# Two chunks of the first batch taking turns by groups of blocks, with sequence sums kept in DRAM between turns

## The chip, the cores and the metric

One core of a Trainium2 chip runs the whole kernel. The metric is the device time of an execution in microseconds (us); a median is over the runs named beside it.

Engines: PE multiplies matrices, PEld loads its weights, DVE is the vector engine, ACT the scalar engine, POOL is GpSimd, SP issues most transfers.

## The reference

A Fourier filter along the sequence, then a gated feed-forward block:

```python
X = np.fft.rfft(x, axis=1)                      # x: (8, 3008, 256) float32
y = np.fft.irfft(X * (filt_r + 1j * filt_i)[None], n=3008, axis=1).astype(np.float32)
h = y.reshape(8 * 3008, 256)
g = h @ w_gate                                  # (256, 1536), float64
silu = g * (1.0 / (1.0 + np.exp(-g)))
return (silu * (h @ w_val) @ w_out).astype(np.float32)
```

The weights arrive as 64-bit floats, 3 x 3.1 MB.

## The kernel before: the parts that matter

For each of 8 batches the kernel does the filter as matrix products (stage 1, stage 2, and stage 3, which writes y) and then the feed-forward block in 12 steps. A step is one chunk k (of 4, in sequence) with one group g (of 3) of the hidden units. In the schedule, tokens such as `Q0`, `A01`, `E23` are groups of products on weights or on sums of weights, and `t0.1` and the like are pieces of the filter for later chunks and the next batch, slipped in between. `t4` is what stage 3 of a chunk reads back from DRAM (tile `t`); `f`, `c` and `m` are copies that ACT makes of PE's results and that PE or DVE needs to go on. The products `A`, `B`, `E` multiply sums of sequence parts ("sequence sums", the tile `y_t`) with sums of weights, so each change of chunk needs new sums, and each change of group other weights.

The 64-bit weights are turned into float32 in 36 half-blocks, one per *round*. A round works on half-block i and finishes half-block i-1:

```python
def round_half(i):
    raw = raws[i]                                 # 128 x 2 x 128 pairs of 32-bit words
    pw = ...; w = ...                             # ring buffers
    DVE: w  = high word & 0xFFFFF                 # "the mask"
    DVE: pw = (high word >> 20) & 0x7FF
    ACT: w, pf, pf, pw                            # four operations, 0.42 to 0.51 us each
    load_weights(i + NRAW - 1)                    # issued by ACT
    yield
    DVE: pw = sign bits | pw;  w = low word * 2**-52 + w
    POOL: products w * pf into the weight tile, then sums of them    # KERNEL BEFORE

def round_next():
    first half of round i, then second half of round i-1
```

(This is shortened; names and order are the kernel's.) Before the steps begin, 17 rounds are done; steps 0, 1 and 2 of the first batch carry 6, 10 and 4 more. Each group of the finished weights is stored to DRAM (3.3 MB) so that later chunks and batches can load them again.

## Time and profile before

| | before |
|---|---|
| time, median of 3 runs | 3012.14 us (3010.92 to 3012.99) |
| PE busy | 97% |
| first feed-forward product (`wk`) starts at | 100.2 us |
| PE restarts after its last long gap at | 125.2 us |
| steps 0, 1, 2, 3, 4 of batch 0 | 53.9, 48.5, 38.8, 30.3, 30.3 us |
| end of step 4 | 302 us |

A step with PE at its limit takes 30.3 us; only the first 241 us have anything to give.

### The profile page before, as it was taken

The page shows a single profiled execution, that of the slowest core. Times are in us where ns is not written, and L with a number is a line of the kernel's source. Part 1 is how long each engine was busy: PE and PEld are TensorE (multiplying, and loading weights), DVE is VectorE, ACT ScalarE, POOL GpSimd, SP SyncE. Part 2 cuts the span into 40 slices and gives each one's busy share as a digit, 9 for nine tenths or more (in the row PEclk, how much of TensorE's full clock was granted, in tenths as well). Part 3 has the DMA queues.
Part 4 walks back from the last instruction along what each step waited for, and adds up shares of the span by engine and source line. Part 5 has one row for each costly group of instructions (what it writes and reads, how often), then busy time and mean ns, then how long its engine had stood idle before and what let it go on. Part 6 is the DMA issues. An engine that isn't in the chain of part 4 may idle for free.

```text
span 3008.6 us, 57532 instructions
## 1 busy us (share of the span) xinstructions
PE 2930.9 (97%) x20286; PEld 2836.1 (94%) x20286; DVE 1920.6 (64%) x4385; ACT 1627.2 (54%) x4206; POOL 1578.4 (52%) x1763
## 2 busy tenths in 40 slices
PE   7589999999999999999999999999999999999999
PEld 5479999999999999999999999999999999999999
DVE  5675676566765666557665576655676566766665
ACT  6565555555555555555555545555545555555554
POOL 3664645455645455546554556544655445654453
PEclk8789999999999999999999999999999999999999
DMA  8445665556655656456655575556664556544442
GB/s 218 138 169 184 214 199 165 185 186 194 212 165 179 207 188 213 150 186 207 198 174 184 173 227 184 182 171 194 197 215 156 188 186 202 193 161 145 139 135 90
DMA packets 203849, 545.53 MB, mean 181 GB/s; under 512 B 28992, under 2 KB 99760, under 8 KB 202704
## 3 DMA queue, kind: packets, MB, share of 16 engines
q1 hardware_dynamic: 153002, 466.50, 48.6%
q10 hardware_dynamic: 41632, 51.46, 5.2%
q0 software_dynamic: 8928, 23.89, 2.6%
q8 instruction: 163, 2.67, 0.4%
q14 instruction: 124, 1.02, 0.1%
HBM read 459.68 MB, written 82.05 MB: 180 GB/s over the span
## 4 chain that ended last, share of the span: by engine, by line
PE 92%; DVE 0%; ACT 0%; issue 0%; POOL 0%; ACTq 0%
PE wa L626 24%; PE wA L703 17%; PE wk L626 16%; PE we L626 12%; PE wG L703 8%; PE wF L703 4%; PE pd L548 3%; PE pa L465 3%; PE pb L505 2%; PE pc L532 2%; DVE o L219 0%; DVE pw L284 0%; DVE y L226 0%; DVE h L222 0%; DVE h L219 0%
## 5 line engine op out<-in xcount | busy, mean ns | idle before, releaser
L626 PE MATMUL wa<-y_t,wt_t 128*128 128x188 f32 x4560 | 900.1, 323 | 5.8 <-ACT m L661 2.7
L626 PEld LDWEIGHTS wa<-y_t,wt_t 128*128 128x128 f32 x4560 | 747.0, 190 | 31.2 <-issue 15.2
L626 PE MATMUL wk<-y,wt_t 128*128 128x188 f32 x3040 | 583.0, 325 | 34.2 <-ACT f L641 24.0
L219 POOL TENSOR_TENSOR h<-h 128x376 f32<-128x376 f32 x190 | 182.7, 984 | 815.9 <-DVE h L673 815.9
L703 PE MATMUL wA<-wo_t,h 128*128 128x128 f32 x4608 | 579.8, 276 | 3.7 <-DVE o L219 2.7
L703 PEld LDWEIGHTS wA<-wo_t,h 128*128 128x128 f32 x4608 | 565.1, 192 | 16.9 <-issue 12.0
L222 POOL TENSOR_TENSOR h<-h 128x376 f32<-128x376 f32 x570 | 553.0, 994 | 0.5
L626 PEld LDWEIGHTS wk<-y,wt_t 128*128 128x128 f32 x3040 | 491.9, 191 | 63.8 <-ACT f L641 25.4
L222 DVE TENSOR_TENSOR we<-we,m 128x376 f32<-128x376 f32 x576 | 319.0, 556 | 202.4 <-PE we L626 145.5
L626 PE MATMUL we<-y_t,wt_t 128*128 128x188 f32 x2280 | 440.5, 323 | 0.0
L626 PEld LDWEIGHTS we<-y_t,wt_t 128*128 128x128 f32 x2280 | 377.5, 190 | 0.1
L222 POOL TENSOR_TENSOR D<-f,f 128x376 f32<-128x376 f32 x288 | 280.2, 986 | 110.0 <-ACT f L641 109.3
L226 DVE SCALAR_TENSOR_TENSOR y<-wk,c 128x376 f32<-128x376 f32 x480 | 244.5, 543 | 141.0 <-ACT we L657 87.0
L661 ACT COPY m<-wa 128x376 f32<-128x376 f32 x576 | 272.2, 473 | 89.9 <-PE wa L626 88.8
L668 ACT ACTIVATE g<-wa 128x188 f32<-128x188 f32 x576 | 188.3, 327 | 196.1 <-PE wa L626 188.4
L703 PE MATMUL wG<-wo_t,h 128*128 128x128 f32 x2304 | 289.5, 276 | 0.6 <-DVE o L219 0.6
L703 PEld LDWEIGHTS wG<-wo_t,h 128*128 128x128 f32 x2304 | 282.7, 192 | 0.8 <-DVE o L219 0.8
L668 ACT ACTIVATE u<-we 128x188 f32<-128x188 f32 x576 | 189.3, 329 | 168.2 <-DVE we L222 149.2
L641 ACT ACTIVATE f<-wk 128x376 f32<-128x376 f32 x288 | 139.7, 485 | 242.2 <-PE wk L626 223.3
L645 ACT COPY c<-wk 128x376 f32<-128x376 f32 x288 | 136.1, 473 | 227.4 <-PE wk L626 227.2
L648 DVE SCALAR_TENSOR_TENSOR x<-wk,f 128x376 f32<-128x376 f32 x192 | 104.4, 544 | 236.8 <-PE wk L626 236.2
L657 ACT COPY we<-y 128x376 f32<-128x376 f32 x480 | 223.6, 487 | 31.3 <-DVE h L673 12.9
(128 smaller groups left out, 3856.3 us busy)
## 6 DMA issues: line engine op xcount, KB each, us to landing
wt_t<-w_all SPq DMA_DIRECT2D x186, 896.0 KB
wt_t<-w_all SPq DMA_DIRECT2D x186, 768.0 KB
t<-d SPq DMA_DIRECT2D x64, 384.0 KB
d<-t ACTq DMA_DIRECT2D x112, 192.0 KB
lent<-de_tbl SPq DMA_DIRECT2D x84, 256.0 KB
lent<-in_filt_r_dram SPq DMA_DIRECT2D x336, 64.0 KB
lent<-d SPq DMA_DIRECT2D x84, 256.0 KB
d<-lent ACTq DMA_DIRECT2D x84, 256.0 KB
```

The source lines that it names most:

```text
L219: return eng.tensor_tensor(out=dst, in0=a, in1=b, op=ALU.add)
L222: return eng.tensor_tensor(out=dst, in0=a, in1=b, op=ALU.subtract)
L226: return nc.vector.scalar_tensor_tensor(out=dst, in0=a, scalar=-1.0, in1=b, op0=ALU.mult, op1=ALU.subtract)
L465: pin(nc.tensor.matmul(out=ps[0:NK], lhsT=wf_t, rhs=self.x.pop(u), start=True, stop=True))
L626: pin(nc.tensor.matmul(out=ps[:, z], lhsT=self.wt[:, SLOT[p], z], rhs=rhs, start=start and z == 0, stop=True, skip_group_check=True))
L641: pin(act.mul(self.small(f"f{i}", f"f{i}", 1), t[f"k{i}"], -1.0))
L645: pin(act.copy(out=self.small(f"c{i}", f"c{i}", 1), in_=t[f"k{i}"]))
L648: pin(v.scalar_tensor_tensor(out=dst, in0=t[f"k{j}"], scalar=-1.0, in1=t[f"f{i}" if j == 3 else f"D{at}"], op0=ALU.mult, op1=ALU.add))
L657: pin(act.copy(out=self.bank(f"e{at}"), in_=t[f"y{at}"]))
L661: pin(act.copy(out=self.small(f"m{at}", "m", 4), in_=t[f"a{at}"]))
L668: pin(act.activation(out=self.small(op, "g", 3, 1)[:, 0], in_=ps[:, 1], func=AF.Silu))
L703: pin(nc.tensor.matmul(out=self.tiles[at][:, t, :], lhsT=self.hs[i][:, HID[p], t0:t0 + 128], rhs=wo_t[:, JB * q + i, WO[p], :], start=star ...
```

## The change

The intent: between two changes of weights there are now two steps instead of one, because chunks 0 and 1 use each group in turn. So group 1 is needed one step later and group 2 two steps later, fewer rounds have to be done before the first step (10 calls in place of 17), and the rest spread evenly (6, 6, 6, 6, 3). The price is that the sequence sums of the two chunks, which share one tile, are stored and loaded again at each turn.

```diff
-    xpool = pool("xp", 3)
+    xpool = pool("xp", 2)
-    NRAW = 3
-    N_EARLY = 16
+    NRAW = 2
+    N_EARLY = 15
-        pw = rpool.tile(..., tag="pw", bufs=2)
+        pw = rpool.tile(..., tag="pw", bufs=3)
-        pin(e.tensor_tensor(out=y, in0=w[:, 1], in1=pf[:, 1], op=ALU.mult))       # e is POOL
+        pin(v.tensor_tensor(out=y, in0=w[:, 1], in1=pf[:, 1], op=ALU.mult))       # v is DVE
  ... (the other two products likewise)
-            if u < N_TWO:                      # real filter part doubled by two ACT copies
+            if u < N_TWO and u % 3:            # four of twelve blocks: two half products on DVE
-        idle(tb0..., [bank("idle") for _ in range(4)], 512)
-        for _ in range(4):
+        for _ in range(2):
             round_next()
  ... (rounds inside the filter loop and behind it: 2 + 1 in place of 5;
       just before the first step 1 in place of 4)
+    yt_dram = [wdpool.tile([128, 3 * len(PAIRS), TQ], FP32, name=f"yt_{k}") for k in range(2)]
+    def keep_sums(k, d):
+        pin(nc.sync.dma_start(out=sums_of(yt_dram[k], d), in_=sums_of(y_t, d)))
+    def reload_sums(k, d):
+        pin(nc.sync.dma_start(out=sums_of(y_t, d), in_=sums_of(yt_dram[k], d)))
+    for d in (2, 1, 3):
+        keep_sums(0, d)                        # behind four weight stores, all on SP
+        if b == 0:
+            steps[:2 * NG] = [(k, g) for g in range(NG) for k in range(2)]
-                if step in (0, 2, 5):
+                chunk = ({0: 1, 2: 2, 5: 3} if b else {0: 1, 3: 2, 6: 3}).get(step)
  ... (t4 of that chunk is loaded at the start of the step)
```

Cut: the new tables of which round, weight sum and filter piece goes to which token, the output tile's second buffer, and the order in which half-blocks are taken.

More of the change, by code (lines that the diff above doesn't have):

```diff
@@ L191, in weights_of @@
     def weights_of(b, k, g):
-        return wt_1 if (b, k, g) == (0, 0, 1) else wt_t
+        return wt_1 if b == 0 and k < 2 and g == 1 else wt_t
     dram_tiles = [wdpool.tile([2 * NS, N2, C], FP32, name=f"d{1 + i % 2}_{i // 2}")
                   for i in range(4)]
+    yt_dram = [wdpool.tile([128, 3 * len(PAIRS), TQ], FP32, name=f"yt_{k}") for k in range(2)]
     w_dram = wdpool.tile([NG, 128, NPR, 2, 128], FP32, name="w_all")
@@ L250, in weight_halves @@
                 yield from hid(g, i)
-            for j in range(JB * (g - 1), JB * g) if g else ():
+            for j in range(JB * g, JB * g + JB):
                 yield from proj(j)
-        for j in range(JB * (NG - 1), NJ):
-            yield from proj(j)
     weights = list(weight_halves())
     raws = {}
-    NRAW = 3
-    N_EARLY = 16
+    NRAW = 2
+    N_EARLY = 15
     def load_weights(i):
@@ L275, in round_half @@
         low, high = raw[:, :, :, 0], raw[:, :, :, 1]
-        pw = rpool.tile([128, 2, 128], U32, name=f"pw_{i}", tag="pw", bufs=2)
+        pw = rpool.tile([128, 2, 128], U32, name=f"pw_{i}", tag="pw", bufs=3)
         w = rpool.tile([128, 2, 128], FP32, name=f"w_{i}", tag="w", bufs=2)
@@ L304, in round_half @@
             dst = wo_t[:, j]
-            pin(e.tensor_tensor(out=dst[:, ts(l, 2), :], in0=w, in1=pf, op=ALU.mult))
+            pin(v.tensor_tensor(out=dst[:, ts(l, 2), :], in0=w, in1=pf, op=ALU.mult))
             if l:
@@ L315, in round_half @@
         x, y, u = w[:, 0], wt[:, SLOT[f"Q{i}"], z], wt[:, SLOT[f"P{i}"], z]
-        pin(e.tensor_tensor(out=y, in0=w[:, 1], in1=pf[:, 1], op=ALU.mult))
-        pin(e.tensor_tensor(out=x if KS[i] else u, in0=x, in1=pf[:, 0], op=ALU.mult))
+        pin(v.tensor_tensor(out=y, in0=w[:, 1], in1=pf[:, 1], op=ALU.mult))
+        pin(v.tensor_tensor(out=x if KS[i] else u, in0=x, in1=pf[:, 0], op=ALU.mult))
         if KS[i] == -1:
@@ L356, in reload_weights @@
         tc.keep_in_program_order(nc.sync.dma_start(out=wt_t[:, a:b], in_=w_dram[g, :, a:b]))
-    PREPARE = {(0, "B03"): [("k", 1, p) for p in range(4)], (1, "B03"): [("k", 2, 0)],
-               (2, "A01"): [("k", 2, p) for p in (1, 2, 3)]}
-    for step, tokens in ((0, "Q0 P3 P0 Q2 A01 B01"), (1, "Q0 P3 P1 A13 P2 B13 Q3 A12 B02 B12"),
-                         (2, "A13 P2 B01 A02")):
+    PREPARE = {(2, "B03"): [("k", 1, p) for p in range(4)], (4, "B03"): [("k", 2, p) for p in range(4)]}
+    for step, tokens in ((0, "Q1 P1 A13 B13 A12 E13"), (1, "Q0 P1 A01 Q3 E12 A23"),
+                         (2, "Q0 P1 A01 Q3 E12 A23"), (3, "Q0 P1 A01 Q3 E12 A23"),
+                         (4, "Q2 B13 E12")):
         for token in tokens.split():
             PREPARE.setdefault((step, token), []).append("r")
-    for g, pairs in ((1, "0Q313 0A0201 0A1202 0B0212 0B1223 0A2303"),
-                     (2, "1A0213 1E1201 1E0202 2Q112 2P123 2Q203")):
+    for g, pairs in ((1, "1E2313 1B0301 2P302 2P012 2P223 2B0103"),
+                     (2, "3E2313 3B0301 4P302 4P012 4P223 4B0103")):
         for p in pairs.split():
@@ L466, in stage1 @@
                                          start=True, stop=True))
-            self.load_x(u + 3)
+            self.load_x(u + 2)
             yield
@@ L510, in stage2a @@
             v = nc.vector
-            fr, fi = (f[:, 0], f[hi, 1]) if self.b else (self.real.pop(u), f[hi])
-            pin(v.tensor_tensor(out=pt, in0=ps, in1=fr, op=ALU.mult))
+            fi = f[hi, 1] if self.b else f[hi]
+            if self.b or u in self.real:
+                fr = f[:, 0] if self.b else self.real.pop(u)
+                pin(v.tensor_tensor(out=pt, in0=ps, in1=fr, op=ALU.mult))
+            else:
+                for h in (lo, hi):
+                    pin(v.tensor_tensor(out=pt[h], in0=ps[h], in1=f[lo], op=ALU.mult))
             pin(v.scalar_tensor_tensor(out=qt[lo], in0=ps[hi], scalar=-1.0, in1=fi,
@@ L571, in stage3, with sums_of @@
                         out=v, in0=b, scalar=-float(k), in1=c, op0=ALU.mult, op1=ALU.add))
+    def sums_of(t, d):
+        a = SUM[f"A0{d}"]
+        return t.rearrange("p (e s) n -> p e (s n)", e=3)[:, :, a * TQ:(a + 4 - d) * TQ]
     def combine_sequence(y, d, v=nc.gpsimd):
@@ L679, in step @@
                 if self.following:
-                    combine_sequence(self.following(), i)
+                    self.following(i)
         def project(self, op, last=False):
@@ L709, in project @@
                 outs[b, k] = [opool.tile([128, len(TOK), C], FP32, name=f"o{i}_{b}_{k}",
-                                         tag=f"o{i}") for i in range(2)]
+                                         tag=f"o{i}", bufs=2) for i in range(2)]
             i, cb = {1: (0, 0), 2: (0, 0), 6: (0, 1), 3: (0, 1), 4: (1, 0), 7: (1, 1),
@@ L757, in early_raw @@
             t = wt_t[:, spare[i]:spare[i] + 2].rearrange("p s z f -> p (s z f)") if i < 8 else \
-                wo_f[:, ts(i - 8, 512)]
+                wo_f[:, JB * 7 * 128 + 512 * (i - 8):JB * 7 * 128 + 512 * (i - 7)]
             return t.bitcast(U32).rearrange("p (b f two) -> p b f two", b=2, two=2)
@@ L776 @@
                 round_next()
-        idle(tb0.rearrange("p s k c -> p (s k c)"), [bank("idle") for _ in range(4)], 512)
         for u in range(2):
@@ L791 @@
                 run(spec.stage2b(u - lag))
-            if 2 < u < 11:
+            if u in (2, 5):
+                round_next()
+            if 2 < u < 9:
                 load_weights(len(raws))
@@ L796 @@
     following = Spectral(1)
-    for u in range(3):
+    for u in range(2):
         following.load_x(u)
-    for _ in range(3):
-        round_next()
+    round_next()
     for i, j in PAIRS:
         combine_weights(0, i, j)
-    for _ in range(2):
-        round_next()
     warm()
@@ L811 @@
         keep_weights(0, piece)
-    for _ in range(4):
-        round_next()
+    round_next()
+    def keep_sums(k, d):
[4 more added lines that the diff above has]
+        keep_sums(0, d)
     hpool = pool("hp", 4)
@@ L822, with order_of, sequence_of, make @@
     pieces_before = []
+    def order_of(b):
+        steps = [divmod(step, NG) for step in range(NCHUNK * NG)]
+        if b == 0:
+            steps[:2 * NG] = [(k, g) for g in range(NG) for k in range(2)]
+        return steps
+    def sequence_of(cur, nxt, step):
+        steps = order_of(cur.b)
+        if step + 1 == len(steps):
+            return (lambda d: combine_sequence(nxt.y[0], d)) if nxt else None
+        k, after = steps[step][0], steps[step + 1][0]
+        if k == after:
+            return None
+        if cur.b == 0 and 0 < step < 2 * NG - 1:
+            return lambda d: reload_sums(after, d)
+        def make(d):
+            combine_sequence(cur.y[after], d)
+            if cur.b == 0 and step == 0:
+                keep_sums(after, d)
+        return make
     for b in range(B):
@@ L846 @@
             plan[10], plan[11] = two[21:24], three(nxt, 0)
+            if b == 0:
+                plan[0], plan[1] = d[0] + one[0:1], one[1:6]
+                plan[4] = [iter(()), iter(())] + two[0:3]
+                plan[5], plan[6] = d[1] + two[3:4], two[4:9]
+                plan[7] = two[9:10] + d[2]
+                plan[8], plan[9], plan[10] = two[10:15], two[15:20], two[20:24]
         else:
@@ L850 @@
         for step in range(NCHUNK * NG + (b == B - 1)):
-            k, g = divmod(step, NG)
             ghost = step == NCHUNK * NG
+            k, g = order_of(b)[min(step, NCHUNK * NG - 1)]
             this = None
@@ L856 @@
                 pieces = plan[step]
-                sequence = None
-                if g == NG - 1 and k < NCHUNK - 1:
-                    sequence = lambda cur=cur, k=k: cur.y[k + 1]
-                elif g == NG - 1 and nxt:
-                    sequence = lambda nxt=nxt: nxt.y[0]
-                this = Group(b, k, g, cur.y[k], sequence)
-                if step in (0, 2, 5):
+                this = Group(b, k, g, cur.y[k], sequence_of(cur, nxt, step))
+                chunk = ({0: 1, 2: 2, 5: 3} if b else {0: 1, 3: 2, 6: 3}).get(step)
+                if chunk:
                     for i in range(2):
-                        cur.load_t4({0: 1, 2: 2, 5: 3}[step], i)
+                        cur.load_t4(chunk, i)
             elif before is None:
@@ L891 @@
                 if b + 2 < B and (step, op) == (9, "B01"):
-                    for u in range(3):
+                    for u in range(2):
                         following.load_x(u)
-                if nxt and (step, op) == (10, "A12"):
+                if nxt and (step, op) == (10, "A12" if b else "E23"):
                     for i in range(2):
@@ L903 @@
                         combine_weights(*a[1:])
-                if op in ends and not last and (b or step > 1):
+                if op in ends and not last and (b or step > 4):
                     reload_weights((g + 1) % NG, ends[op])
```

## The prediction

> **What bounds the kernel now.** First the page's busy table and slices (75 us each), to find where PE, the matmul engine, is not the limit.
>
> ```profile
> PE 2930.9 (97%) x20286; PEld 2836.1 (94%) x20286; DVE 1920.6 (64%) x4385; ACT 1627.2 (54%) x4206; POOL 1578.4 (52%) x1763
> ...
> PE   7589999999999999999999999999999999999999
> ...
> PEclk8789999999999999999999999999999999999999
> ```
>
> PE is full in 37 of 40 slices; only the first three, about 225 us, have holes, and there the granted clock is low as well. Next the windows view, cut where the schedule's steps start (a step starts where the W2 products of the group before it run): steps 0, 1, 2 of the first batch, then steps 3 and 4. Columns: window, length, busy us (instructions) of PE, PEld, DVE, ACT, POOL; granted clock, DMA share, GB/s.
>
> ```profile
> 100.20:154.10 53.90, 27.70 (x127) 23.96 (x128) 37.04 (x87) 36.02 (x86) 33.96 (x53) 0.74 0.35 113
> 154.10:202.60 48.50, 39.08 (x211) 35.08 (x210) 36.35 (x87) 34.85 (x86) 30.39 (x48) 0.82 0.34 114
> 202.60:241.40 38.80, 33.29 (x206) 30.01 (x205) 28.65 (x60) 21.61 (x55) 29.11 (x37) 0.96 0.70 230
> 241.40:271.70 30.30, 30.30 (x201) 27.76 (x200) 17.34 (x41) 16.27 (x43) 12.24 (x15) 1.00 0.49 158
> 271.70:302.00 30.30, 30.30 (x226) 30.20 (x225) 17.86 (x43) 17.19 (x43) 13.75 (x18) 1.00 0.62 199
> ```
>
> A step that PE bounds takes 30.3 us; steps 0 to 2 take 53.9, 48.5 and 38.8. They carry 6, 10 and 4 rounds of the weight preparation, each of which splits one half-block of 64-bit weights and rounds it. No engine is full: the busiest, DVE, has 69%, 75% and 74%. So these steps are bound by in-order queues waiting for each other. Third, PE's own waits in the first 240 us:
>
> ```profile
> PE wk L626 <- ACT f L641: 28.8, 5, 19.8
> PE wpb L505 <- ACT room L495: 11.5, 1, 11.5
> PE wk L626 <- DVE y L219: 10.2, 1, 10.2
> ```
>
> Columns: total us, times, longest. In the timeline the first long gap ends at 49.9 (four rounds stand in ACT's queue before the copy that PE needs), the second at 100.2 (two rounds stand before the first y copies), the third at 125.2 (four more before the first f). After 241 us the waits view gives PE 1.5 us of waits in all. Hence only the time up to 241.4 can be won. A step 0 without projections needs some 21 us, 30.3 less the 84 x 0.11 us of projections.
>
> **What the Trainium skill says.** "Perfetto Trace Analysis", section Sequencer Loop: an engine reads its instructions one after another; I take from the trace that a stalled one holds up the later ones (19.8 us on f while PE had work behind it). "SBUF — State Buffer", section Who interferes with whom: a DVE tensor_scalar in a two-port mode and a GpSimd operation exclude one another for a whole instruction. The trace agrees: the masking op at L282 takes 0.27 us alone and up to 1.12 beside POOL's work. "TensorE: Matmul & The Clock Gate", section What's actually happening: idle time lowers PE's clock. The trace agrees: 0.74 and 0.82 in the holed steps, so a gap costs more than its length (PE was busy 39.1 us in step 1 for work that takes 30.3). "DMA: Bandwidth & Descriptors", section Anatomy of one DMA: about 2 us are fixed per transfer; the profile lists issues, so I use it only as an estimate.
>
> **The change, part by part.**
> (1) Fewer rounds before step 0: 10 calls in place of 17, then 6, 6, 6, 6, 3 in steps 0 to 4 in place of 6, 10, 4. Group 1 of the weights is needed at step 2 rather than 1, group 2 at step 4 rather than 2, since chunks 0 and 1 share each group in turn.
> (2) The multiplications of a round move from POOL (2 x 0.46 us, or 0.78) to DVE. By the other 256-column DVE operations (0.41 to 0.45) I count 0.45. A round then costs DVE 2.03 (0.556 + 0.585 + 0.466 + 0.426), less about 0.25 of port contention, plus 0.45: 2.2 us. ACT keeps 0.417 + 0.500 + 0.508 + 0.416 = 1.84 (1.71 end to end) plus 0.38 for issuing the load. DVE's next mask no longer waits for POOL's product; those waits (8.1 + 9.4 + 5.3 us before the three L282 groups) mostly go. pw's third buffer helps the same way.
> (3) Four filter blocks skip two ACT copies each (8 x 0.62 = 5.0 us off ACT) and pay one more half-height DVE product (4 x 0.69 = 2.8 us).
> (4) The idle matmuls on the table go: 5.75 us of PE just before the transposes.
> (5) The sums: y_t holds 128 x 18 x 188 floats, 1.73 MB. Two copies out and four back are 10.4 MB; three weight reloads of 3.33 MB fall away. DMA stays even, with a share of 0.34 to 0.7 here.
> (6) x gets two buffers, not three; raw two, not three; the outputs two.
>
> Start-up, by the old timeline. The fourth round leaves ACT at 30.5 as before; two t2 copies (1.0), four filter copies (2.5) and two rounds (3.4) end at 37.5, so DVE starts the filter products at about 37 in place of 48.2. The loop took 27.3 us of DVE; with (3) and two rounds inside it, 27.3 + 2.8 + 3.6 = 33.7, so it ends at 71 in place of 75.5 (if DVE keeps its pace, nearer 70). Last stage-2b copy about 3.8 us later, warm matmuls 7.8, wpd 3.7: PE reaches the first wk at 85 in place of 100. POOL makes the B and E weights (9.3 us) until 82 to 83, then six of the sums (6.6 us) until 92. Only then may SP issue the last sums' write, and the t4 load of chunk 1 stands behind it. That matters because chunk 1's first stage-3 product is now at t0.0, right after Q0, in PE's queue. Behind about 2.5 MB (1.73 of sums, 0.79 of t4) at the 300 GB/s or so seen while the old kernel stored its weights, that is 8 us, and the t4 lands at about 98 to 100. PE waits from 85 to 99, but the old one restarted at 125.2. Gain here 26 us, less a microsecond or two because more of Q0 to P0 was already done there.
>
> Steps 0 to 4. DVE's own work is 16.5 to 17.5 us a step (17.34 and 17.86 above), 13.5 in step 0. Six rounds add 13.2; a weight combination adds 0.55 or 1.6, so two add 2.1 and four 4.3. DVE: 27, 32, 34, 32 and, with three rounds and the first stage-2 pieces, 30 us. ACT: 16.3 + 6 x 2.1 + 1.7 for issuing the d stores = 30.6 us in steps 1 to 3. Both stand at or over PE's 30.3, so PE does not bound these steps. At 85 to 90% of the fullest engine, better than the old 75% because (2) cuts DVE's tie to POOL, they take about 30, 36, 38, 36 and 33 us: 173. From 99 that ends at 272; counting the rest of the old step-0 front, 273. The old kernel is there at 302.0 (end of step 4). From there both run the same PE-bound schedule, with the same tail. Saving about 29 to 33 us; a DVE total gives a check: about 191 us busy to 300 us before, 205 with the added products; from 28 us on at 82% with the t4 hole it ends near 270. I take 32: 3012 - 32 = 2980.
>
> **Rivals.**
> A: the sums' round trip becomes the wait. For: t4, x loads and reloads share one in-order SP queue, and the 3.4 MB weight stores stand before the d=3 reload. Against: the d=1 reload (0.87 MB) has about 12 us from n1 to A01 and d=2 about 18; d=3 is used late. If true, each of four steps loses 3 to 5 us: 2995 to 3000.
> B: PE becomes the bound at once and DVE and ACT pack perfectly. Then steps take 22 + 4 x 31 from 95: end at 241, saving 61: 2951. Against: ACT at 30.6 and DVE at 32 to 34 in in-order queues.
> C: two x buffers starve stage 1 in every batch. A load has two slots of about 6 us instead of three; a 0.9 MB weight piece ahead takes 4 to 5. For: seven batches pay, so 2 us each step with stage 1 would be 40 us: 3020. Against: PE waited for no x at all after 241 us.
> D: the start gains nothing, as the t4 chain eats it, and the steps stretch to 40: 2998.
>
> **Range and chances.** The largest thing to win is 302.0 less an ideal 228 (85, then 22 and four of 30.3), 74 us or 2.5%; 2% needs 60 of them, which takes rival B. Range 2956 to 3001. Faster by over 2%: 0.05; within 2%: 0.94; slower: 0.01.
>
> **What would show it.** In the new profile: DVE's first filter product near 37 us; first wk near 85; a PE wait for a DMA (t4) of 10 to 15 us ending near 99; DVE and ACT at 85% or more in steps 1 to 3; each of these 34 to 39 us with PE waits split over many small ones on ACT and DVE; clock above 0.9 there; later steps 30.3 as before. Wrong if PE waits for y_t loads (A) or x (C), or if steps 1 to 3 take 31 (B), or if the first wk is not before 95.

## The result, and the profile after

The changed kernel took 3021.22 us (median of 4 runs, 3019.97 to 3023.83); the kernel before, on the same chip, 3012.56 us (4 runs). The ratio is 1.0029, with a 95% interval of 1.0011 to 1.0046. (A ratio here compares the fast runs of both kernels in the same rounds, so it is not quite the ratio of the medians.) That is 41 us above the prediction, outside its range, and on the wrong side: a loss of 0.3% and no gain of 1.1%.

Busy totals, slices of PE and slices of its clock in the changed kernel, as the prediction shows them for the kernel before:

```profile
PE 2943.7 (97%) x20278; PEld 2844.6 (94%) x20278; DVE 1947.2 (64%) x4449; ACT 1624.1 (54%) x4198; POOL 1548.8 (51%) x1703
...
PE   7688999999999999999999999999999999999999
...
PEclk7899999999999999999999999999999999999999
```

The thin part is no shorter, it only has another shape: the second to fourth slices are 6, 8, 8 where they were 5, 8, 9. The steps show why. Windows of the changed kernel from the restart of PE: steps 0 to 4 (columns: window, length, busy us (count) of PE, PEld, DVE, ACT, POOL; granted clock, DMA share, GB/s):

```profile
108.20:146.50 38.30, 29.18 (x138) 26.91 (x139) 22.70 (x63) 25.50 (x62) 12.62 (x15) 0.80 0.15 47
146.50:187.40 40.90, 34.68 (x200) 30.48 (x198) 31.91 (x79) 28.65 (x75) 18.43 (x25) 0.92 0.44 132
187.40:230.70 43.30, 35.31 (x201) 30.08 (x200) 32.80 (x75) 27.18 (x69) 21.89 (x29) 0.92 0.42 121
230.70:275.70 45.00, 34.52 (x200) 29.97 (x199) 31.16 (x80) 25.98 (x65) 16.31 (x22) 0.92 0.64 208
275.70:312.30 36.60, 31.84 (x201) 29.83 (x200) 33.29 (x67) 17.14 (x45) 23.18 (x30) 0.95 0.45 127
```

PE restarts 17 us earlier than before (108.2 against 125.2), and then gives all of it back and more: five steps take 204 us where 173 were predicted, and step 4 ends at 312.3, not 273, and not 302.0 as in the kernel before. DVE's busy times are those predicted to within 3.3 us in steps 1 to 4 (31.9, 32.8, 31.2, 33.3 against 32, 34, 32, 30). So DVE's work was counted right (ACT's was counted high, 30.6 us against 26.0 to 28.7 in steps 1 to 3); the steps are longer than the work. DVE, the fullest engine beside PE itself, has 78, 76 and 69% in steps 1 to 3, where 85 to 90% had been assumed.

PE's waits in the first 300 us of the changed kernel (total us, times, longest):

```profile
PE pd L552 <- DMA t<-d: 13.8, 1, 13.8
PE wa L634 <- ACT m L669: 11.1, 8, 3.9
PE wk L634 <- ACT f L649: 10.1, 6, 4.4
```

The first is the predicted wait for t4, with nearly the predicted length. The others are ACT's copies, late. Why they are late is to be looked for one engine further back, in what ACT and DVE wait for in steps 0 to 3 (a line of each engine's waits):

```profile
ACT w L285 <- DVE w L281: 25.7, 15, 6.9
```

```profile
DVE w L281 <- DMA raw<-in_moe_w_gate_dram: 6.4, 2, 6.0
```

L281 is the mask, DVE's first operation of a round; L285 is ACT's first. ACT stood 25.7 us in front of a round whose mask DVE had not come to. In the kernel before the same pair, over steps 0 to 2 with the restart at 125.2, is 13.5 us in 14 times, 1.9 at the longest, and DVE's mask has no wait for raw there among its largest.

The one wait of 6.0 us for raw can be followed to PE. It makes the longest wait of PE in step 3, 5.1 us (three lines of the timeline: start, duration, engine, operation; in brackets the idle time before it and what ended it):

```profile
234.26 0.37 ACTq L268 DMA_DIRECT2D raw<-in_moe_w_gate_dram  x1
243.09 0.29 DVE L281 TENSOR_SCALAR w<-raw 128x256 uint32<-128x256 uint32 x1 [5.97 <-DMA raw<-in_moe_w_gate_dram]
245.40 2.90 PE L711 MATMUL wA<-wo_t,h 128*128 128x128 f32 x12 [5.14 <-POOL wt_t L220]
```

The profile names POOL for PE's wait, but that POOL operation waited for DVE's product of the same round, behind the mask. The load was issued at 234.3, just after SP had issued the four stores of group 1 (228.6 to 231.3), and took 8.8 us to arrive.

Of the 38 us by which steps 1 to 3 exceed three times 30.3, PE waits for 25; in the rest it is busy longer than 30.3 us a step, at a granted clock of 0.92. The clock alone is not what sets the length: in no_sums (below) it was 1.00 in step 1, which took 40.8 us all the same.

After step 4 the rest of the batch loses some 3 us more: steps 5, 6 and 10 take 1.0, 0.8 and 0.9 us longer than before, and the new plan gives steps 5 and 10 one filter piece more each. From the second batch on all steps are alike.

### The profile page after: what moved, and what is told of

Same layout as the page of the kernel before. It is cut to its first block, busy times and chain, and to the rows that moved or that the text cites. A ratio compares the mean times of both kernels' runs of the same rounds, so it can differ in the third digit from the quotient of the medians.

```text
span 3022.0 us, 57521 instructions
## 1 busy us (share of the span) xinstructions
PE 2943.7 (97%) x20278; PEld 2844.6 (94%) x20278; DVE 1947.2 (64%) x4449; ACT 1624.1 (54%) x4198; POOL 1548.8 (51%) x1703
## 4 chain that ended last, share of the span: by engine, by line
PE 90%; DVE 1%; ACT 0%; issue 0%; ACTq 0%; DVEq 0%
PE wa L634 23%; PE wA L711 16%; PE wk L634 15%; PE we L634 12%; PE wG L711 8%; PE wF L711 4%; PE pd L552 3%; PE pa L464 3%; PE pc L536 2%; PE pb L504 2%; DVE o L220 0%; DVE h L681 0%; DVE y L227 0%; DVE pw L294 0%; DVE w L297 0%
## 5 line engine op out<-in xcount | busy, mean ns | idle before, releaser
L634 PEld LDWEIGHTS wa<-y_t,wt_t 128*128 128x128 f32 x4512 | 741.7, 191 | 34.1 <-issue 16.9
L634 PE MATMUL wk<-y,wt_t 128*128 128x188 f32 x3008 | 576.6, 325 | 9.0 <-ACT f L649 9.0
```

The lines of the kernel that those rows point to most:

```text
L634: pin(nc.tensor.matmul(out=ps[:, z], lhsT=self.wt[:, SLOT[p], z], rhs=rhs, start=start and z == 0, stop=True, skip_group_check=True))
```

## The experiments

Each kernel below gave the right result unless it says otherwise, and each was timed in rounds with the kernel before on the same chip, except the two marked "one look". Chips differ between experiments; the median of the kernel before was 3012.06 to 3013.25 us on them. The labels are explained below in turn. Step starts are the first product of `wF` in a step, and steps are read from one profile of each kernel.

| kernel | median us | ratio to before (95%) | PE restart | steps 0, 1, 2, 3, 4 |
|---|---|---|---|---|
| changed | 3021.22 | 1.0029 (1.0011 to 1.0046) | 108.2 | 38.4, 41.0, 43.2, 45.0, 36.7 |
| t4_first | 3012.85 | 1.0002 (0.9987 to 1.0017) | 91.3 | 43.1, 40.6, 43.1, 45.5, 36.6 |
| fine | 3040.68 | 1.0095 (1.0078 to 1.0112) | 106.7 | 37.3, 46.6, 47.8, 51.1, 38.9 |
| no_sums (wrong result) | 3017.87, one look | | 101.4 | 38.9, 40.8, 43.2, 45.4, 36.9 |
| fake_rounds (wrong result) | 2971.31, one look | | 105.9 | 26.4, 30.8, 30.2, 36.6, 30.2 |
| five_raws | 3005.43 | 0.9977 (0.9963 to 0.9992) | 94.8 | 41.8, 38.2, 42.0, 41.4, 36.6 |
| lag | 3001.61 | 0.9963 (0.9948 to 0.9978) | 95.3 | 41.0, 36.6, 40.2, 40.6, 36.7 |
| muls_pool | 3013.04 | 1.0003 (0.9986 to 1.0019) | 94.5 | 42.6, 39.2, 44.3, 43.7, 36.8 |
| fring | 3013.85 | 1.0007 (0.9992 to 1.0022) | 93.8 | 42.8, 40.5, 43.1, 45.7, 36.7 |
| lag_pool | 2997.99 | 0.9948 (0.9934 to 0.9961) | 91.1 | 41.2, 37.0, 40.0, 40.7, 36.7 |
| stores | 2994.97 | 0.9940 (0.9926 to 0.9953) | 93.5 | 41.1, 36.6, 40.3, 34.6, 36.6 |
| combo | 2994.70 | 0.9937 (0.9924 to 0.9951) | 92.2 | 42.3, 36.4, 40.1, 34.8, 36.7 |
| lag8 | 2991.56 | 0.9929 (0.9912 to 0.9945) | 93.7 | 34.5, 37.3, 40.2, 35.3, 36.7 |
| split | 2987.25 | 0.9911 (0.9897 to 0.9926) | 91.0 | 36.4, 36.1, 39.3, 34.0, 36.6 |

One caution for reading it: the restart differs by up to 4 us between kernels whose start is the same (t4_first 91.3, lag 95.3, stores 93.5), as the start of the filter loop (38.6 to 40.9 us) and its length (35.0 to 38.5) vary from profile to profile. So differences of the median under 4 us are judged by the steps' lengths, which repeat to a few tenths (compare t4_first and fring, whose steps are the same).

### The wait for t4

```diff
+    for i in range(2):
+        spec.load_t4(1, i)                 # ahead of the stores of weights and sums
     for piece in range(len(PIECES)):
         keep_weights(0, piece)
-  chunk = ({0: 1, 2: 2, 5: 3} if b else {0: 1, 3: 2, 6: 3}).get(step)
+  chunk = ({0: 1, 2: 2, 5: 3} if b else {3: 2, 6: 3}).get(step)
```

> The changed kernel with chunk 1's two t4 loads issued ahead of the stores of weights and sums instead of behind them; the result stays right. Theory W (the 13.8 us wait of PE at 108 us is the SP queue's order: the load stands behind the last sums' store) expects that wait to fall below 3 us and the restart to come near 98 us; if nothing else takes its place the time falls by about 10 us, to 3011. Theory Q (every round costs some 2.7 us of the path wherever it stands) allows the same. Rival: round ten and the copies behind it take the wait's place and less than 4 us are won, 3018.

The wait fell to one of 1.2 us:

```profile
PE pd L552 <- DMA t<-d: 1.2, 1, 1.2
```

PE restarted 16.9 us sooner (some 4 of it the start's spread: the first `wk` came at 89.3 in place of 93.6), the span of the profiled run fell by 12.2 us and the median by 8.4. Not all of it arrived because step 0 grew from 38.4 to 43.1 us: it now begins while DVE and ACT still finish the start, and PE waits 10.2 us in it for ACT's copy f (4.4 before), as the rival said in kind. The loads stand in SP's in-order queue, so this cure is an order of issue and costs nothing. "DMA: Bandwidth & Descriptors", section Queues, rings and completion order, in the Trainium skill says that each DMA engine consumes the descriptors of a ring in ring order. No run here shows rings by themselves; what the trace shows is the order of issue. In the changed kernel SP issued the sums' stores from 99.3 us on, when POOL had made the sums, and the t4 loads only at 102.1, so 7.7 of the 13.8 us passed before their issue.

### The sums' round trip

```diff
     def keep_sums(k, d):
-        pin(nc.sync.dma_start(out=sums_of(yt_dram[k], d), in_=sums_of(y_t, d)))
+        pass
     def reload_sums(k, d):
-        pin(nc.sync.dma_start(out=sums_of(y_t, d), in_=sums_of(yt_dram[k], d)))
+        pass
```

> The changed kernel without any store or reload of the sequence sums; the result is wrong on purpose. Theory S (the sums' round trip through DRAM is what eats the gain) expects steps 1 to 4 to fall by 5 us each, about 2995. Theories Q and O expect steps 1 to 4 to stay within 2 us of 41, 43, 45, 37, and only the start to gain 3 to 8 us because the t4 load no longer stands behind the sums' stores: 3013 to 3018.

The steps kept their lengths (40.8, 43.2, 45.4, 36.9), though the DMA share in step 1 fell from 0.44 to 0.29. So the stores and loads of the sums, the part of the change that looks dearest, cost nothing in the steps. Their first store cost 5 us of the t4 wait (8.7 us left of 13.8), which t4_first takes away as well.

### Are the rounds the whole excess?

```diff
+    def fake_round():       # clears the round's weights with POOL, no load, no DVE, no ACT
-                        round_next()
+                        fake_round()
```

> The changed kernel with the rounds of steps 0 to 4 replaced by a memset of the same places on POOL; the result is wrong on purpose. Theories Q and O expect steps 1 to 4 at 30 to 32 us each, step 0 shorter by 10 us or more, in all about 55 us less: near 2965. Theory S expects steps 1 to 4 to stay above 36 us because the sums still travel: near 2995.

Windows of the kernel without the rounds' work, steps 0 to 4:

```profile
105.90:132.30 26.40, 25.16 (x139) 23.95 (x140) 14.16 (x36) 16.78 (x42) 10.97 (x17) 0.87 0.12 37
132.30:163.10 30.80, 30.50 (x200) 27.80 (x200) 16.50 (x43) 18.11 (x48) 18.32 (x32) 1.00 0.42 127
163.10:193.30 30.20, 30.20 (x199) 27.65 (x198) 19.76 (x44) 17.67 (x45) 18.18 (x31) 1.00 0.41 123
193.30:229.90 36.60, 32.09 (x200) 28.87 (x199) 18.14 (x45) 15.90 (x41) 15.00 (x25) 0.95 0.65 212
229.90:260.10 30.20, 29.08 (x203) 28.23 (x202) 25.53 (x54) 13.69 (x37) 19.69 (x25) 1.00 0.53 147
```

Three of the four whole steps (1 to 4) are at PE's limit. The exception, step 3, holds one wait of PE for x of 4.5 us, and will come back below. The five steps take 154.2 us in place of 204.3, so 27 rounds cost 50 us, 1.9 each. The prediction's 173 us, against 143 for steps that PE bounds (22 and four times 30.3), had allowed 1.1 each. The kernel before spent 58.6 us over the same limit in steps 0 to 2 (141.2 us against 82.6). Of these, 19.8 are the one wait for f before its restart, which the prediction puts down to four of the early rounds. The other 39 make 1.9 for each of its 20 rounds. By this estimate a round became no cheaper by the change, and seven more of them stand in the steps.

### Finer slices

The first theory of why a round is dear was that it puts a lump into each in-order queue. The edit cut a round into four slices, one every five tokens: the two masks; two of ACT's operations; the other two; the load with the second half of the round before.

```diff
         pin(v.tensor_scalar(out=pw, in0=high, scalar1=20, ...))
+        yield
         pin(nc.scalar.activation(out=w, in_=man, ...))
         pin(nc.scalar.activation(out=pf, in_=pw, ..., bias=off_t))
+        yield
         pin(nc.scalar.activation(out=pf, in_=pf, ..., bias=top_t))
         pin(nc.scalar.activation(out=pw, in_=pf, ...))
+        yield "half"
         load_weights(i + NRAW - 1)
```

> The changed kernel with each round of steps 0 to 4 cut into four slices (DVE masks; two ACT operations; two ACT operations; load and the second half) that are issued at tokens five apart instead of all at one token. Same operations, same order among themselves, right result. Theory Q (a round's block of some 2.1 us in ACT's in-order queue, with its wait for DVE, delays what PE waits for) expects steps 1 to 4 to lose about half of their excess over 30.3 us (45 us in all), so 3000 or less. Theory O (DVE and ACT have too much work, the products moved from POOL to DVE above all) expects no change within 5 us: 3016 to 3026, since the amount of work is the same.

It was slower by 19 us, and the steps took 46.6, 47.8, 51.1 and 38.9 us. The expectation failed, but the waits say that the slices also moved the load later. DVE's waits of this kernel in steps 0 to 3:

```profile
DVE w L281 <- DMA raw<-in_moe_w_gate_dram: 15.0, 5, 8.7
DVE w L281 <- DMA raw<-in_moe_w_out_dram: 13.5, 5, 4.1
```

In the changed kernel the first of these is 6.4 us and the second 0.8. With two buffers, a load is issued only one round ahead; put some tokens later it came too late 12 times (the ten above, and two for the third weight, 2.6 us). So the run told nothing on lumps, but it pointed at the raw buffers.

### Raw buffers

By count a third raw buffer of the pool does not fit beside the second output buffer that the change needs (no run shows it). But three slices of the projection weights of the last group are free until half-block 32, so five buffers can serve in turn, with loads three rounds ahead. (This and all later kernels include t4_first.)

```diff
-        if i < N_EARLY:
-            raws[i] = early_raw(i)
+        if i < N_EARLY or (i - N_EARLY) % 5 > 1:
+            raws[i] = early_raw(i if i < N_EARLY else 10 + (i - N_EARLY) % 5)
-        load_weights(i + NRAW - 1)
+        load_weights(i + AHEAD)            # AHEAD = 3
```

> t4_first with five buffers in turn for the raw halves (two of the pool and three slices of the projection weights of group 2, which nothing uses before half 32) and each load issued three rounds ahead in place of one, into a buffer whose last reader was done a round ago. In t4_first DVE waited 6.7 us for raw in steps 1 to 4 (one wait of 6.2) and ACT's first operation of a round waited 22.7 us for DVE's mask, 7.1 of it in the same place. Theory R (the raw loads, issued one round ahead and behind the weight stores, are a good part of what a round costs): the raw waits are gone and steps 1 to 4 lose 6 to 9 of their 165.8 us, so about 3005. Rival H (what costs is that ACT's part of a round stands in its queue until DVE has come to the mask): about 14 us of ACT's waits for the mask stay, the time falls by 3 us at most, 3010 or more.

DVE's waits for raw are gone from its list for steps 1 to 3 (6.7 us in t4_first), and the steps 1 to 3 fell from 129.2 to 121.6 us, by 7.6; the median by 7.4. The expectation of theory R held. What rival H said of the remaining waits held too: ACT still waited 18.8 us for the mask in these steps (22.7 in t4_first), so both causes are there. Two things this run leaves open. Three buffers, as in the kernel before, were not tried. And 6.2 of the 6.7 us are one wait in step 3, in which group 1 is being stored, so spreading those stores (below) might have cured it too; that was not tried with two buffers.

### The hand-over from DVE's mask to ACT

```diff
-                        round_next()
+                        round_dve()            # mask of i, rest of i-1
+                        due.append(at + LAG)   # LAG = 3: ACT's four operations and the load three tokens later
```

> five_raws with one thing more: in steps 0 to 4 ACT's part of a round (four operations and the load's issue) comes three tokens of the schedule after DVE's part (masks of this half, rest of the half before), so that the mask is made before ACT asks for it. Work and order on each engine's own list of rounds stay the same. Theory H (the hand-over from DVE's mask to ACT inside one token): ACT's waits for the mask fall from some 14 us to under 5, steps 1 to 4 take 33 to 35 us each in place of 41, and the time is 2990 to 2998. Rival Q (ACT's and DVE's own blocks of 2 us in the in-order queues delay the copies that PE needs, wherever they stand): the time stays within 3 us of five_raws, the waits of PE for ACT the same.

ACT's waits for the mask in steps 1 to 4 fell from 21.7 to 12.7 us, not under 5, and steps 1 to 3 from 121.6 to 117.4 us, 4.2 less. Theory H had promised 33 to 35 us a step, and got 36.6, 40.2, 40.6, 36.7. So the hand-over is a cause, but a small one.

### Where the products are done

```diff
-        pin(v.tensor_tensor(out=y, in0=w[:, 1], in1=pf[:, 1], op=ALU.mult))
+        pin(e.tensor_tensor(out=y, in0=w[:, 1], in1=pf[:, 1], op=ALU.mult))
  ... (and the other two)
```

> t4_first with the products of a round back on POOL, as the kernel before has them; pw keeps its three buffers. The prediction took this part of the change for the one that raises the occupancy. If so, steps 1 to 4 grow by 0.2 to 0.4 us a round, 3016 to 3022, with waits of DVE's masks for POOL's products back. Rival O (the products on DVE, 0.9 us a round or so, make DVE's queue the longer one): faster by 4 to 10 us, 3003 to 3009.

> lag with the products of a round back on POOL. In lag DVE was busy 33.0 of 36.6 us in step 1, 33.3 of 40.2 in step 2, 31.3 of 40.6 in step 3 (4.3 of them a wait of PE for x) and 33.4 of 36.7 in step 4, that is 83 to 91% of the time; the products are about 0.55 us of DVE in each of 21 rounds, 11.5 us. Theory D (with the raw waits and the hand-over gone, DVE's own work sets the length of these steps): steps 1 to 4 lose 7 to 11 of their 154.1 us, 2991 to 2995. Rival O (the in-order hand-over to POOL and the port that DVE shares with it cost what DVE saves, as muls_pool against t4_first hinted): within 3 us of lag, or slower, 2999 to 3006.

muls_pool stands on t4_first. Its steps 1 to 3 took 127.2 us against 129.2; the time was the same within the intervals. lag_pool stands on lag, where DVE was fuller. Steps 1 and 3 of lag, then of lag_pool:

```profile
136.30:172.90 36.60, 33.01 (x201) 29.62 (x200) 32.97 (x80) 28.41 (x74) 18.58 (x25) 0.95 0.51 150
...
213.10:253.70 40.60, 33.92 (x200) 30.16 (x199) 31.29 (x80) 25.75 (x65) 16.42 (x23) 0.87 0.69 223
```

```profile
132.30:169.30 37.00, 33.03 (x201) 29.39 (x200) 28.52 (x69) 28.41 (x74) 23.18 (x35) 0.95 0.50 147
...
209.30:250.00 40.70, 33.48 (x200) 29.72 (x199) 26.15 (x66) 25.29 (x64) 22.05 (x34) 0.92 0.70 223
```

DVE is relieved of 4.5 and 5.1 us and the steps are as long as before (154.1 and 154.4 us for four). Its median is 3.6 us lower only because it restarted 4.2 us earlier, which is the spread of the start. So theory D fell: taking 5 us of work off DVE, even at 90%, does not shorten these steps. (That POOL's larger share costs just as much, as rival O has it, is not excluded.) The waits of DVE's masks for POOL's products, which should have come back, were 0.2 us in muls_pool and 0.3 in lag_pool over steps 1 to 4. So the part of the change that the prediction credited with a better occupancy, the move of the products to DVE, is worth nothing that these runs can show, either way.

### The wait for x

In lag, as in fake_rounds (4.5 us) and five_raws (3.4), PE waited for x in step 3; in the changed kernel, where PE stood 5.1 us in step 3 behind the load of raw, it did not:

```profile
PE pa L477 <- DMA x<-in_x_dram: 4.3, 1, 4.3
```

Ahead of that load, in SP's queue, stand the four stores of group 1 and then the two t4 loads of chunk 2. Between the stores and the t4 loads SP stood for 6.6 us, which its own waits put down to the stores.

```diff
-    PREPARE = {(2, "B03"): [("k", 1, p) for p in range(4)], ...
+    PREPARE = {(2, "B03"): [("k", 1, 0)], (3, "P3"): [("k", 1, 1)], (3, "Q2"): [("k", 1, 2)],
+               (3, "Q3"): [("k", 1, 3)], ...
```

> lag with the four pieces of group 1's weight store, 3.3 MB, no longer issued together at the end of step 2 but one there and three spread over step 3. In lag PE waited once 4.3 us for x in step 3, right behind these stores in the in-order SP queue; the kernel with false rounds had the same wait (4.5 us). Theory: the x wait goes, step 3 falls from 40.6 to some 36.5 us and the time to 2997. Rival: the wait moves (to the next x load or to DVE's own work, as when t4 was loaded first), and the time stays at 3000 to 3002.

> All that is thought to help together: chunk 1's t4 loaded first, five raw buffers, ACT's part of a round three tokens late, products on POOL, stores of group 1 spread. If both theories of the two runs before hold, 2987 to 2991; if DVE's products don't matter, 2997. In either case faster than the kernel before by 0.5 to 0.8%.

The wait went, and step 3 fell from 40.6 to 34.6 us, more than the wait: PE was also busy 2.5 us less in it, with the granted clock at 1.00 in place of 0.87:

```profile
211.50:246.10 34.60, 31.45 (x199) 27.76 (x199) 31.17 (x80) 25.52 (x65) 16.42 (x22) 1.00 0.82 262
```

The transfers did not shrink; the share of DMA is 0.82. They only stopped standing in front of an input. Whether the third x buffer, which the change also gave up, would have bridged the wait was not tried. combo adds the products on POOL and is no faster than stores (2994.70 and 2994.97), above what was expected if both helped, and so a third sign that the products' place does not matter here.

### What is left: distance or lumps

In step 2 of stores, the longest wait of PE for ACT's copy m (2.6 us, ending at 188.74) looks like this (start, duration, engine, operation; in brackets the idle time before it and what ended it):

```profile
184.65 1.07 DVE L283 TENSOR_SCALAR w<-wo_t 128x256 uint32<-128x256 uint32 x1
...
185.63 0.81 DVE L285 TENSOR_SCALAR pw<-wo_t 128x256 uint32<-128x256 uint32 x1
185.74 0.42 ACT L288 ACTIVATE w<-w 128x256 f32<-128x256 uint32 x1 [3.37 <-DVE w L283]
...
186.37 0.94 DVE L297 SCALAR_TENSOR_TENSOR pw<-wo_t,pw 128x256 uint32<-128x256 uint32 x1
186.48 0.51 ACT L290 ACTIVATE pw<-pw,off_t 128x256 f32<-128x256 uint32 x1 [0.32 <-DVE pw L285]
...
187.02 0.51 ACT L291 ACTIVATE pw<-pw,top_t 128x256 f32<-128x256 f32 x1
187.23 1.20 DVE L300 SCALAR_TENSOR_TENSOR w<-wo_t,w 128x256 f32<-128x256 uint32 x1
187.56 0.42 ACT L292 ACTIVATE pw<-pw 128x256 uint32<-128x256 f32 x1
187.57 0.38 ACTq L270 DMA_DIRECT2D wo_t<-in_moe_w_gate_dram  x1
```

Two things stand here one behind the other. ACT waits 3.4 us for the mask, and then its four operations occupy it from 185.7 to 188.0 while the copy m, which PE waits for, stands behind them. DVE's operations are themselves long (1.07, 0.81, 0.94 and 1.20 us, where the same lines take 0.28, 0.28, 0.41 and 0.41 when POOL is idle). That agrees with "SBUF — State Buffer", section Who interferes with whom, in the Trainium skill, which the prediction names: it also counts DVE operations with two inputs in SBUF, as the last two are, among those that contend with POOL's reads. Two kernels took the two things apart, both on stores:

```diff
+    LAG = 8                 # lag8: ACT's block eight tokens after DVE's part, not three
```

```diff
+    LAG = (4, 8)            # split: two operations after four tokens, two and the load after eight
         pin(nc.scalar.activation(out=pf, in_=pw, func=AF.Relu, bias=off_t))
+        yield
         pin(nc.scalar.activation(out=pf, in_=pf, func=AF.Relu, bias=top_t, scale=-1.0))
```

> stores with ACT's part of a round eight tokens after DVE's part in place of three (seven where the next round follows sooner). In stores ACT still waited 3.4 us for a mask in step 2, because DVE's mask came 1.1 us late and took 1.07 us beside POOL, and PE then waited 2.6 us for the copy m behind the round's four operations. Theory H: with more distance these waits go too, steps 1 to 4 lose 3 to 6 of their 148.1 us, 2989 to 2992. Rival Q (the block of 2.2 us that a round puts into ACT's queue delays the copies wherever it stands): steps 1 to 4 within 2 us, waits of PE for m as long as before.

> stores with ACT's part of a round in two blocks of two operations, four and eight tokens after DVE's part (the load's issue with the second). Theory Q: blocks of 0.9 and 1.3 us in place of 2.2 halve the longest waits of PE for ACT's copies; steps 1 to 4 fall by 4 to 8 us and by at least 2 us more than with lag8. Rival H: the same as lag8 within 1.5 us. If neither kernel gains, what is left of the steps' excess is spread over PE's clock and small waits, and stays open.

With lag8, ACT's wait for the mask is no longer among its seven largest, and yet steps 1 to 4 took 149.5 us (148.1 in stores), as the rival expected. (PE's waits for the copy m did fall, from 6.5 to 4.2 us, but those for ACT's copy `wa` rose from 2.8 to 6.6.) Its gain is in step 0 (34.5 us for 41.1), where two rounds stand only seven tokens apart (14 or more in steps 1 to 3). With split the four steps took 146.0 us, 3.5 less than lag8 and 2.1 less than stores, so the expected 2 us beyond lag8 are there, the expected 4 to 8 us below stores are not. Nor were the longest waits for ACT's copies halved: the longest for m is 2.5 us in split, 2.6 in stores and 2.2 in lag8, and all of PE's waits for ACT in steps 1 to 4 are 10.6, 12.0 and 12.5. Distance changed together with the size of the blocks (four and eight tokens, against three or eight). So a small gain is there; that the smaller lump makes it is likely and not shown. Windows of split, steps 0 to 4:

```profile
91.00:127.40 36.40, 25.98 (x138) 24.21 (x139) 32.03 (x76) 28.02 (x71) 19.33 (x25) 0.86 0.52 189
127.40:163.50 36.10, 32.47 (x201) 28.04 (x200) 32.99 (x80) 27.71 (x74) 19.53 (x26) 1.00 0.54 161
163.50:202.80 39.30, 33.29 (x199) 29.17 (x199) 33.50 (x75) 26.27 (x68) 22.21 (x30) 0.96 0.45 131
202.80:236.80 34.00, 31.88 (x201) 27.82 (x200) 31.22 (x81) 24.90 (x65) 16.45 (x23) 1.00 0.81 261
236.80:273.40 36.60, 31.58 (x202) 29.80 (x201) 33.29 (x67) 17.12 (x45) 23.21 (x30) 0.95 0.42 127
```

This kernel ends step 4 at 273.4, and at 2987.25 us it beats both the kernel before (by 0.9%) and the changed one.

### A miss at the start

```diff
-                self.real[u] = early("fr", u)
+                self.real[u] = early("fr", u - u // 3 - 1)
```

> t4_first with the three buffers for the doubled real filter used in turn by all eight blocks that still have a copy (in the changed kernel the number of the block picks the buffer, and as every third block has no copy only two buffers serve). Theory: ACT's copies waited there for DVE's product of the block before, held the t2 copies behind them, and PE's stage 2b and DVE waited 5.4 us in the loop; the loop shrinks by 4 to 5 us from its first product to its last, and the time is 3008 or so. Rival: the loop is bound by DVE and POOL's port or PE anyway and the time stays at 3012 to 3013.

In the filter loop of the changed kernel DVE waited 5.4 us for PE. Every third block skips its copies, but the block's number still picks one of three buffers, so only two serve. With all three in use the loop did not shrink: from DVE's first filter product to the start of its last it took 37.1 us, against 35.0 to 38.5 in the other kernels with this start. ACT's two largest waits between 28 and 100 us, in t4_first:

```profile
ACT y_t L529 <- DVE room L513: 7.6, 6, 2.2
ACT w L285 <- DVE w L281: 6.2, 4, 4.5
```

and in fring:

```profile
ACT x L540 <- PE wpc L536: 12.4, 8, 3.5
ACT w L285 <- DVE w L281: 7.3, 4, 4.5
```

The wait for the buffer went and a wait for PE's products of stage 2b came in its place. The theory fell.

## Why the prediction was wrong, point by point

In the profiled runs the miss is made of 9 us in the start, 31 in steps 0 to 4 and 3 in the rest of the first batch, which the prediction took as unchanged ("with the same tail").

**The bound before** was read rightly: in the changed kernel fake_rounds shows three of the steps at 30.2 to 30.8 us once the rounds' work is gone, and all but those 3 us was won or lost before 312 us. One reading of the lines was off: "the busiest, DVE, has 69%, 75% and 74%" passes over PE, busy 81 and 86% of steps 1 and 2, and POOL, 29.1 us in step 2 against DVE's 28.7.

**Start-up.** "DVE starts the filter products at about 37": 40.8, in a spread of 38.6 to 40.9 over the kernels with this start. The loop of 33.7 us was sized without its own waits and took 38.5 to the start of its last product. So the first `wk` came at 93.6, not at 85. This is a term mis-sized by 9 us (4 in the loop's start, the rest in the loop); that fring did not shorten the loop leaves open what holds it.

**The t4 wait.** "PE waits from 85 to 99": it waited 13.8 us, to 108.2. Its length and cause were right, its place was late with the start. The prediction took it as given; t4_first shows that an earlier issue of two loads avoids it.

**The parts of the sum.** DVE's busy time per step was right within 3.3 us, ACT's was 2 to 5 us too high, and the finding that the sums' transfers (rival A) would be hidden was right: no_sums. Two x buffers (rival C) starve nothing in later batches; but in the first, once the wait for raw is cured, one x load stands behind a 3.3 MB store, for 3.4 to 4.5 us.

**The step that failed** is this one: "At 85 to 90% of the fullest engine, better than the old 75% because (2) cuts DVE's tie to POOL, they take about 30, 36, 38, 36 and 33 us: 173." The fuller of DVE and ACT had 78, 76 and 69% in steps 1 to 3, and the five steps took 204. What the runs show in its place:
- The raw loads: 7.6 us (five_raws). The change takes raw from three buffers to two. The prediction lists that in part (6) and gives it no cost. This is its plainest omission, though that three would have been enough was not tried.
- The x load behind the stores of group 1: 6.0 us in step 3 (stores).
- The hand-over from mask to ACT: 4.2 us with a small distance (lag), and 6.6 more in step 0 with a larger one (lag8).
- ACT's part of a round in two blocks: 2.1 us in steps 1 to 4 against stores, 3.5 against lag8 (split); that the lump is the cause is not shown.
- Reason (2), the products' move, is worth nothing measurable (lag against lag_pool, stores against combo). The trace of the kernel before says why: of the 22.8 us for which its masks waited for POOL (the 8.1 + 9.4 + 5.3 of part (2)), 18.7 lie before PE's restart at 125.2, and only 4.0 in the stretch from there to the end of step 2. The tie that was to be cut was not what held those steps.

With all these cured steps 1 to 4 take 146.0 us in place of 165.9, where 143 were predicted; with DVE at 91, 85, 92 and 91%. Some 25 us over four times 30.3 remain; fake_rounds puts them down to the rounds, and no run here splits them further. So the figure of 85 to 90% describes a schedule that has had these waits removed, not the one that the diff contained. The percentage was chosen from the direction of one part of the change and not from a list of what each round waits for.

**The rivals.** None was right as told. D, "the start gains nothing, as the t4 chain eats it, and the steps stretch to 40", came nearest: the steps stretched beyond 40, but the start did gain 17 us at the restart. Its 2998 does not follow from its words: from a restart at 125 and with four steps of 40 us the time would be some 3020 by an estimate from the old kernel's times, about what was measured.

**What stays open.** Steps 2 and 4 of split still take 39.3 and 36.6 us. Step 4 took 36.6 to 36.9 us in every kernel but fine (38.9) and fake_rounds (30.2), though it has only three rounds: neither raw buffers, distance, lumps nor the products' place touch it. Both steps, 2 and 4, hold four weight combinations besides the rounds. The combinations alone are not the reason, as fake_rounds has them too; whether the two together are was not tried.

## What to carry to other kernels

A busy share of 75% in a stage that no engine bounds is not a reserve that a new schedule will use. List the waits that each inserted piece of work brings (its input load, its hand-over between engines, what stands behind it in each in-order queue), and price every buffer that the change takes away. If a diff lowers a buffer count to make room, look first at how far ahead the load of that buffer could be issued before and after. And order transfers in an in-order queue by who waits for them: two small loads moved ahead of stores, and stores spread behind loads, were worth 8 and 7 us here without any work being removed.

## What the Trainium skill lacked or had wrong

- "Trainium Kernel Development and Optimization", section Best Practices, says to double-buffer. Here two buffers for raw were not enough: five with loads three rounds ahead took 7.6 us off three steps (three or four were not tried). The page has no word on how to tell how far ahead a load must be issued.
- "DMA: Bandwidth & Descriptors" tells of ring order, but not what follows for a kernel when an input load is issued behind stores whose data are not ready or not yet moved. The runs show 13.8 us (t4 behind weights and sums) against 1.2, and 4.3 us (x behind 3.3 MB).
- "SBUF — State Buffer", section Who interferes with whom, is right in kind, but its factors come from other measurements, none of them of these operations: a round's four DVE operations took 1.07, 0.81, 0.94 and 1.20 us beside POOL, against 0.28, 0.28, 0.41 and 0.41 alone.
- No page has a way to estimate what work slipped into in-order queues costs beyond its own time: 27 rounds cost 50 us of PE's path, 1.9 us each, in the changed kernel, though DVE was at most 78% busy in steps 1 to 3, and ACT 70%.
